# Attention and mixture of experts in one kernel: another order for the steps of each head pair

## The chip, the cores and the metric

One Trainium2 chip, one of its cores. The metric is the device time of one execution in microseconds (us), as the median of several runs. The kernel before takes 621.43 us (three runs, 620.74 to 623.72).

## What is computed

The reference, cut to what matters: an attention over 4 batches of 8 heads, 576 positions and 64 channels, with a position bias from a small network that is the same for all batches, and behind it a layer of 8 experts of which each token uses one.

```python
scores = scale * np.matmul(q, k.transpose(0, 1, 3, 2))     # q, k, v: (4, 8, 576, 64)
scores = scores + bias.transpose(2, 0, 1)[None, :, :, :]
attn = softmax(scores)
x = np.matmul(attn, v)  ->  (2304, 512)
e_idx = np.argmax(x @ w_gate, axis=1)
for e in range(8):
    mask = e_idx == e
    h = np.maximum(x[mask] @ w1[e], 0.0)                   # w1: (8, 512, 1024)
    out[mask] = gate_w[mask, None] * eom[mask, e, None] * (h @ w2[e])
```

## The kernel before, in words

The program has three stages, one behind the other: the position bias, the attention, and the experts. Each engine executes its instructions in the order in which the program emits them; nothing reorders them, and an instruction that waits holds up all that stand behind it on its engine.

**Attention.** The work goes by pairs of heads: 16 pairs, four to a batch. The code calls the index of the pair n (0 to 15, and 16 for what is left over). A pair is cut into small steps, and the order of the steps is written out by hand in four strings at the top of the file: ORDER (pairs 1 to 14), FIRST (pair 0), LAST (pair 15), END (what is left). A program loop walks through the string and emits one step per word. A minus behind a word means that the step belongs to the pair before, a plus to the next pair, two plus signs to the one after it. The words are:

- `s0` to `s4`: the score matmuls of one block of 128 queries (L833, into PSUM tiles `ps`, of which there are two; a block of two heads takes both, `s4` takes one). `m0` to `m4`: their softmax: VectorE adds the bias and finds the maximum (L845, into `e`), ScalarE takes the exponential (L850).
- `t00` to `t04`, `t10` to `t14`, `t20`, `t21`: TensorE turns pieces of `e` (L886, L898; into PSUM tiles `pt`, three of them), and the letter behind names the engine that copies the result to `et` (L890, L901): `a` is ScalarE, `d` is VectorE.
- `a0`, `a1`, `a2`: the products with the values (L918, one PSUM tile `pa`), with the copy to `xt` (L919) on the engine that the letter names.
- `k0` to `k2` and `h0` to `h2`: keys and queries of the next pair are turned (L810), copied in a high part (L813, ScalarE) and a low part (L815, VectorE, under `h`).
- `l`, `v`, `b`: loads of keys with queries (`nat`), values (`vt`) and the tail of the values (`vb`), issued on SyncE's queue. `z`, `c`, `g`: small copies on GpSimd: the queries of the last block into `q4` (L821), which `s4` reads, and pieces of values into `vz` (L803, L794), which `a0`, `a1`, `a2` read. The very first `t` step also emits the `c` of pair 0 (emit_t).
- `w` and `u`: one step of mixed-in work if there is any: the gate logits of a finished batch (emit_logits), the choice of its expert (emit_route), storing its rows of x (emit_x), and, for the first three batches, the sorting of the tokens by expert (route_group: L415 is its last matmul, L461 writes the indices `gidx`).

In pair 15 the experts begin to move in: `W` loads the first w1 (2 MB), `y` splits half a row block of it into a high part (ScalarE, L539) and a low part (GpSimd, L540), eight in all, `X` first emits what is left of route_group and then the three gathers of the first slot's 288 tokens (first_x, gather, L497: indirect DMAs of 96 rows of 2 KB on GpSimd's queue), and the fourth `y` emits the three gathers of the next slot. The first w2 (first_w2, another 2 MB, L483) is put at the head of the mixed-in work by `m3`. `x` turns a quarter of the gathered tokens (L515), which needs all three gathers.

**Experts.** Eight slots and more of 288 tokens each: matmuls with w1 (L1102) and w2 (L1123).

```python
for n in range(len(pairs) + 1):
    for op in orders.get(n, ORDER).split():
        name = op.rstrip("+-")
        m = n + op.count("+") - op.count("-")
```

Of the kernel before, what the change touches and what calls it, by code (L numbers as in the profile page):

```python
# [20 lines left out]
B, H, S, D = 4, 8, 576, 64  # L21
# [23 lines left out]


ORDER = (
    "l++ s0 b- c t10a- w t12a- m0 u t13d- k2+ s1 u t14a- m1 h2+ u t21d- a0d- w u w u w g- s2 z t20a- t01a t03a m2 u "
    "t02d u a2d- w s3 u k1+ k0+ t00a m3 u s4 w m4 u t04a h1+ h0+ u a1d- v+ t11d u "
)  # L50

FIRST = (
    "l++ s2 z m2 t01a t03a t02d s3 m3 t00a v+ s4 m4 t04a t11d"
)

LAST = (
    "b- B W s0 c t10a- u w t12a- m0 u t13d- u s1 t14a- m1 u t21d- a0d- w u s2 z t20a- g- m2 a1a- u t01a t03a w u y "
    "t02d u s3 y t00a m3 u X y t04d s4 y a2d- m4 w y t11d t13a y a0d u t14d t12a y y w t21d u t20d u "
)

END = (
    "t10a- x x a1d- x x a2d- "
)


BEGIN = {
    3: "k0", 4: "k1", 5: "k2 l", 13: "K0", 16: "K1", 17: "s00", 20: "K2",
    22: "s10 s01", 32: "s11", 35: "v",
}


ON_ACT = "210210000111121212102110310010201111"

# [1176 lines left out]
```

## Time and profile before

| what | value |
|---|---|
| median of three runs | 621.43 us |
| the profiled execution's own time | 626.37 us |
| its span, first to last instruction | 624.6 us |
| TensorE (PE) busy | 580.3 us, 93% |
| VectorE (DVE) busy | 410.8 us, 66% |
| ScalarE (ACT) busy | 362.0 us, 58% |
| GpSimd (POOL) busy | 105.6 us, 17% |
| the chain that ended last, share of TensorE | 79% |

The profile was taken in one execution, and times in it count from its first instruction. In that execution the bias lasts to about 82 us, the attention to about 381 us, the experts to the end. The clock of TensorE that a row gives as 1.00 is 2.4 GHz, as 0.50 it is 1.2 GHz.

### The profile page before, as it was taken

The page shows a single profiled execution, that of the slowest core. Times are in us where ns is not written, and L with a number is a line of the kernel's source. Part 1 is how long each engine was busy: PE and PEld are TensorE (multiplying, and loading weights), DVE is VectorE, ACT ScalarE, POOL GpSimd, SP SyncE. Part 2 cuts the span into 40 slices and gives each one's busy share as a digit, 9 for nine tenths or more (in the row PEclk, how much of TensorE's full clock was granted, in tenths as well). Part 3 has the DMA queues.
Part 4 walks back from the last instruction along what each step waited for, and adds up shares of the span by engine and source line. Part 5 has one row for each costly group of instructions (what it writes and reads, how often), then busy time and mean ns, then how long its engine had stood idle before and what let it go on. Part 6 is the DMA issues. An engine that isn't in the chain of part 4 may idle for free.

```text
span 624.6 us, 13990 instructions
## 1 busy us (share of the span) xinstructions
PE 580.3 (93%) x5294; PEld 472.9 (76%) x5294; DVE 410.8 (66%) x975; ACT 362.0 (58%) x773; POOL 105.6 (17%) x220
## 2 busy tenths in 40 slices
PE   5887899999999999999998979999999999999993
PEld 2333477767777667777676757999999999999993
DVE  6987567666876668766788644766778674655521
ACT  5796677666666676575657563544555455454510
POOL 1000011100011101011104272040404041331202
PEclk9997899999999999999999998999999999999998
DMA  6865653332133332233320565467566575747621
GB/s 144 217 175 143 171 112 68 67 69 57 36 111 76 67 69 58 81 73 67 69 79 28 173 209 171 147 204 240 159 217 199 169 205 174 227 145 236 181 76 44
DMA packets 94997, 81.40 MB, mean 130 GB/s; under 512 B 71319, under 2 KB 71575, under 8 KB 94920
## 3 DMA queue, kind: packets, MB, share of 16 engines
q1 hardware_dynamic: 88932, 66.05, 39.0%
q0 software_dynamic: 3232, 9.64, 4.8%
q10 hardware_dynamic: 2756, 4.72, 2.1%
q8 instruction: 43, 0.70, 0.5%
q14 instruction: 34, 0.28, 0.1%
HBM read 60.34 MB, written 9.50 MB: 112 GB/s over the span
## 4 chain that ended last, share of the span: by engine, by line
PE 79%; DVE 6%; DMA 4%; ACT 4%; issue 3%; POOL 2%; SPq 1%; POOLq 0%; DVEq 0%; ACTq 0%
PE p L1102 16%; PE p L1123 16%; PE pa L918 14%; PE ps L833 10%; PE pt L886 9%; PE pb L737 4%; PE pt L810 2%; DMA bias<-evl 2%; PE pt L515 1%; PE pt L1142 1%; PE pt L898 1%; PE pt L657 1%; DMA xg<-x_dram,gidx 1%; DVE hid L726 1%; DVE e L845 1%
## 5 line engine op out<-in xcount | busy, mean ns | idle before, releaser
L845 DVE CUSTOM_DVE_ANT_0 e<-ps,bias 128x576 f32<-128x576 f32 x144 | 103.9, 754 | 40.1 <-PE ps L833 34.6
L850 ACT ACTIVATE e<-e,nm 128x576 f32<-128x576 f32 x144 | 111.1, 780 | 10.0 <-DVE nm L845 10.0
L1102 PE MATMUL p<-x,w 128*128 128x288 f32 x768 | 105.8, 297 | 0.0
L1102 PEld LDWEIGHTS p<-x,w 128*128 128x128 f32 x768 | 102.8, 188 | 0.5 <-issue 0.4
L886 PE MATMUL pt<-kept,e 128*128 128x128 f32 x576 | 84.1, 280 | 3.6 <-DVE x L666 2.5
L890 ACT COPY et<-pt 128x512 f32<-128x512 f32 (+1 forms) x117 | 59.8, 534 | 42.4 <-PE pt L886 41.0
L886 PEld LDWEIGHTS pt<-kept,e 128*128 128x128 f32 x576 | 62.6, 141 | 20.0 <-issue 9.9
L1123 PE MATMUL p<-hh,w2h 128*128 128x288 f32 x256 | 77.3, 302 | 0.0
L1123 PE MATMUL p<-hl,w2h 128*128 128x288 f32 x256 | 75.6, 295 | 0.1
L1123 PE MATMUL p<-hh,w2l 128*128 128x288 f32 x256 | 75.3, 294 | 0.0
L918 PE MATMUL pa<-et,vt 128*64 128x256 f32 (+1 forms) x640 | 74.9, 360 | 0.0
L737 PE MATMUL pb<-hid,w2blk 128*32 128x288 f32 x576 | 47.9, 459 | 16.7 <-DVE hid L726 7.5
L918 PEld LDWEIGHTS pa<-et,vt 128*64 128x64 f32 x640 | 43.3, 139 | 22.7 <-issue 9.0
L1067 POOL DMA_INDIRECT out_dram<-y,sidx x22 | 26.4, 1198 | 180.5 <-DVE y L1145 154.2
L1104 ACT ACTIVATE hh<-p 128x288 fp32r<-128x288 f32 x64 | 26.3, 411 | 46.3 <-PE p L1102 30.8
L726 DVE TENSOR_SCALAR hid<-e,early 128x576 f32<-128x576 f32 x110 | 48.4, 514 | 7.1 <-PE pb L737 3.5
L737 PEld LDWEIGHTS pb<-hid,w2blk 128*32 128x32 f32 x576 | 19.4, 120 | 41.5 <-DVE hid L726 9.7
L833 PE MATMUL ps<-qt 64*128 64x288 f32 x256 | 47.8, 344 | 2.9 <-DVE nm L845 2.0
L1123 PEld LDWEIGHTS p<-hh,w2h 128*128 128x128 f32 x256 | 48.0, 188 | 0.6 <-issue 0.6
L487 DVE TENSOR_TENSOR w2l<-w2r,w2h 128x1024 fp32r<-128x1024 f32 x32 | 39.2, 1225 | 14.0 <-ACT w2h L486 12.5
L1123 PEld LDWEIGHTS p<-hl,w2h 128*128 128x128 f32 x256 | 48.1, 188 | 0.3 <-DVE hl L1105 0.3
L1123 PEld LDWEIGHTS p<-hh,w2l 128*128 128x128 f32 x256 | 48.2, 188 | 0.0
(222 smaller groups left out, 968.8 us busy)
## 6 DMA issues: line engine op xcount, KB each, us to landing
w1r<-in_moe_w_dram SPq DMA_DIRECT2D x36, 512.0 KB, 5.1
w2r<-in_moe_w_dram SPq DMA_DIRECT2D x36, 512.0 KB, 5.0
bias<-evh SPq DMA_DIRECT2D x16, 288.0 KB, 4.4
bias<-evl SPq DMA_DIRECT2D x16, 288.0 KB
vt<-in_v_dram SPq DMA_DIRECT2D x16, 288.0 KB, 3.4
nat<-in_k_dram SPq DMA_DIRECT2D x32, 128.0 KB, 3.6
nat<-in_q_dram SPq DMA_DIRECT2D x32, 128.0 KB, 2.6
x_dram<-x ACTq DMA_DIRECT2D x12, 256.0 KB, 2.0
```

The costliest lines, as they stand in the source:

```text
L487: V.tensor_tensor(out=lo, in0=src, in1=hi.bitcast(F32), op=ALU.subtract)
L726: V.tensor_scalar(out=to, in0=src, scalar1=bc[:, r:r + 1], scalar2=0.0, op0=ALU.add, op1=ALU.max,)
L737: nc.tensor.matmul(pb[32 * t:32 * t + 32, c, 0:288], lhsT=w2f, rhs=hids[t][:, c * 288:c * 288 + 288], start=True, stop=True,)
L833: nc.tensor.matmul(outs[hl][:, c, 0:288], lhsT=qs[p, S + 64 + qb * 128:S + 192 + qb * 128] if qb < 4 else q4[:, t, :], rhs=keys[p, c * 288 ...
L845: V.tensor_tensor_reduce(out=e.rearrange("p (a j) -> p a j", a=2), in0=ps[:, :, 0:n], in1=bias_ap.rearrange("p (a j) -> p a j", a=2), scal ...
L850: nc.scalar.activation(out=e, in_=e, func=ACTF.Exp, scale=-1.0, bias=nm, accum_out=sum_ap)
L886: nc.tensor.transpose(pt[:, n * 256 + j * 128:n * 256 + j * 128 + 128], es[j][:, (n0 + n) * 128:(n0 + n) * 128 + 128], ident,)
L890: copy(out=et[:, n0:n0 + nn, :].rearrange("p n s -> p (n s)"), in_=pt[:, 0:nn * 256])
L918: nc.tensor.matmul(pa[p:p + 64, 0:n], lhsT=values, rhs=weights, start=i == 0, stop=i == 4)
L1067: p = nc.gpsimd.indirect_dma_start(out=out, out_offset=bass.IndirectOffsetOnAxis(ap=idx, axis=0), in_=y[0:n], in_offset=None, bounds_check ...
L1102: nc.tensor.matmul(p1[:, 0:CH], lhsT=w[:, fs], rhs=x[:, c, :], start=n == 0, stop=n == 11)
L1123: nc.tensor.matmul(p2[:, 0:CH], lhsT=w[f // 2][:, f % 2, ds], rhs=x[f], start=n == 0, stop=n == 23)
```

## The change

The four strings are written anew; no step is added or dropped, and each step does what it did. The line numbers of the rest of the file fall by one. Shortened:

```diff
 ORDER = (
-    "l++ s0 b- c t10a- w t12a- m0 u t13d- k2+ s1 u t14a- m1 h2+ u t21d- a0d- w u w u w g- s2 z t20a- t01a t03a m2 u "
+    "b- w s0 u g- w k1+ k2+ m0 z h2+ a0a- h1+ t21d- u c t20a- u t13a- w t14a- s1 t11a- t10a- m1 w t12d- u "
+    "u l++ k0+ s2 m2 w h0+ w u a1a- s3 t00a m3 t04d u t02a s4 t03a m4 t01d a2a- v+ u "
...
 FIRST = (
-    "l++ s2 z m2 t01a t03a t02d s3 m3 t00a v+ s4 m4 t04a t11d"
+    "l++ t04d s2 t03a m2 t02d z t00a s3 m3 v+ s4 t01a m4 "
...
 LAST = (
+    "a1a- s3 m3 y t00a w t04d t02d s4 t10a t01d t03a y u m4 a2d- X u y y y a0d y t21d u t14a t13a y u u "
...
 END = (
-    "t10a- x x a1d- x x a2d- "
+    "x a1a- x x x a2a- "
```

What moves, in words. In pairs 1 to 14 all copies of `a0`, `a1`, `a2` go from VectorE to ScalarE. The keys of the next pair are turned right behind `s0` and in front of `s2`, no longer beside `s3`; `a0` comes in front of `s1`, and `a1` between `s2` and `s3`. All five `t1` steps of a pair are now emitted in the pair behind it. In pair 0 a `t` step comes first and the `q4` copies (`z`) behind it. In pair 15 `X` stands behind `s4`, `m4` and `a2`, where it stood ahead of `s4`, and the sorting of tokens has four steps left when `X` is reached, where it had none.

GpSimd at the start of the attention, before (`vz` and `et` are cleared, `q` is `q4`, of pair 0; then the values of pairs 0 and 1):

```order
L977 MEMSET vz_897 128x64
L821 CAST q_122<-qt_118 64x64 x2
L821 CAST q_122<-qs_120 64x64 x2
L803 COPY vz_895<-vt 64x64 x2
L803 COPY vz_896<-vt 64x64 x2
```

and now:

```order
L976 MEMSET vz_897 128x64
L802 COPY vz_895<-vt 64x64 x2
L820 CAST q_122<-qt_118 64x64 x2
L820 CAST q_122<-qs_120 64x64 x2
L793 COPY vz_897<-vb 64x64
```

The copies of values of pair 0 stand ahead of the `q4` copies of pair 0, which stood ahead of them.

ScalarE in pairs 2 and 3, from the last exponentials of a pair into the next, before (`e_139` is `m3`, `e_893` is `m4`, `e_136` is `m0`):

```order
L850 ACTIVATE e_139,sums<-e_139,nm 128x576 x2
L850 ACTIVATE e_893,sums_535<-e_893,nm 128x576
L890 COPY et<-pt 128x256
L890 COPY et<-pt 128x512 x2
L850 ACTIVATE e_136,sums<-e_136,nm 128x576 x2
```

and now:

```order
L849 ACTIVATE e_139,sums<-e_139,nm 128x576 x2
L889 COPY et<-pt 128x512 x2
L849 ACTIVATE e_893,sums_535<-e_893,nm 128x576
L918 COPY xt_1225<-pa 128x64
L812 CAST qt_119<-pt 128x384 x2
L849 ACTIVATE e_136,sums<-e_136,nm 128x576 x2
L918 COPY xt_1046<-pa 128x256
```

The copies of `a2` and `a0` (`xt`) and two castings of keys have come into this stretch.

GpSimd in pair 15, before (`w_1` is the low part of w1, written by a `y`; the first two DMA rows are the gathers of the first slot, the third those of the next):

```order
L540 TENSOR_TENSOR w_1_4856<-w1r_4679,w_0_4855 128x512
L540 TENSOR_TENSOR w_1_4856<-w1r_4680,w_0_4855 128x512
L497 DMA xg_4908<-x_dram,gidx_102 96x512 x2
L497 DMA xg_4909<-x_dram,gidx_102 96x512
L540 TENSOR_TENSOR w_1_4856<-w1r_4681,w_0_4855 128x512
L540 TENSOR_TENSOR w_1_4856<-w1r_4682,w_0_4855 128x512
L497 DMA xg_4909<-x_dram,gidx_102 96x512 x3
```

and now:

```order
L539 TENSOR_TENSOR w_1_4765<-w1r_4622,w_0_4764 128x512
L399 TENSOR_TENSOR ge<-ge 128x5x39
L401 TENSOR_TENSOR a_4808<-ge,kept 128x5x39 x2
L539 TENSOR_TENSOR w_1_4765<-w1r_4623,w_0_4764 128x512
L539 TENSOR_TENSOR w_1_4765<-w1r_4624,w_0_4764 128x512
L465 COPY ids_p<-ids_a 96x21
L496 DMA xg_4944<-x_dram,gidx_102 96x512 x2
L496 DMA xg_4945<-x_dram,gidx_102 96x512
L539 TENSOR_TENSOR w_1_4765<-w1r_4625,w_0_4764 128x512
L496 DMA xg_4945<-x_dram,gidx_102 96x512 x3
```

Three `y` steps and the last of the sorting stand ahead of the first gathers, where two `y` steps stood.

## Rows read from the trace of the kernel before

**Rows 1.** Windows: stretch and length, busy PE, PEld, DVE, ACT, POOL, PEclk, DMA, GB/s.

```profile
136.15:211.10 74.95, 73.02 (x712) 54.70 (x713) 52.98 (x139) 48.60 (x123) 7.69 (x35) 1.00 0.31 73
211.10:286.05 74.95, 73.01 (x712) 54.69 (x713) 52.98 (x139) 48.60 (x123) 7.63 (x35) 1.00 0.30 72
286.05:346.70 60.65, 55.14 (x529) 40.43 (x529) 45.38 (x142) 36.92 (x92) 10.77 (x36) 1.00 0.18 48
...
364.55:381.40 16.85, 13.31 (x99) 8.07 (x98) 5.90 (x15) 6.84 (x16) 12.02 (x11) 0.80 0.88 296
```

**Rows 2.** Chain of waits: start, length, what; the products a1 of two pairs.

```profile
119.54 2.31 PE pa L918 x20
...
136.15 2.31 PE pa L918 x20
```

**Rows 3.** Timeline of TensorE in one pair: start, length, tile, shape, count.

```profile
131.18 0.66 PE L886 MATMUL pt<-kept,e 128*128 128x128 f32 x4
131.77 0.40 PE L833 MATMUL ps<-qt 64*128 64x288 f32 x2
...
132.76 1.53 PE L886 MATMUL pt<-kept,e 128*128 128x128 f32 x12
134.14 0.55 PE L810 MATMUL pt<-kept,nat 128*128 128x128 f32 x3
134.62 0.40 PE L833 MATMUL ps<-qt 64*128 64x288 f32 x2
```

**Rows 4.** Groups by form: count, busy us, mean ns, idle before; copies of ScalarE.

```profile
L890 ACT COPY et<-pt 128x512 f32<-128x512 f32 x87 | 48.7, 591 | 41.7 <-PE pt L886 40.4 <-PE pa L918 0.8
L813 ACT CAST qt<-pt 128x384 fp32r<-128x384 f32 x48 | 21.5, 479 | 10.6 <-PE pt L810 10.6
L919 ACT COPY xt<-pa 128x256 f32<-128x256 f32 x1 | 0.4, 372 | 0.2 <-PE pa L918 0.2
```

**Rows 5.** Timeline at the start of the attention, in brackets the wait and its releaser.

```profile
75.25 0.52 POOL L821 CAST q<-qt 64x64 fp32r<-64x64 f32 x2
...
79.25 0.52 POOL L803 COPY vz<-vt 64x64 f32<-64x64 f32 x2 [2.89 <-DMA vt<-in_v_dram]
...
82.19 0.61 SPq L769 DMA_DIRECT2D nat<-in_q_dram  x1
...
84.36 0.52 PE L810 MATMUL pt<-kept,nat 128*128 128x128 f32 x3 [0.86 <-DMA nat<-in_q_dram]
```

**Rows 6.** Two windows of 2 us at the end of the bias, columns as before.

```profile
68.00:70.00 2.00, 1.16 (x20) 0.71 (x24) 0.78 (x3) 0.87 (x2) 0.00 (x0) 0.95 0.79 195
70.00:72.00 2.00, 2.00 (x24) 0.92 (x20) 0.00 (x0) 0.74 (x1) 0.00 (x0) 0.50 0.03 8
```

**Rows 7.** Timeline at the end of the attention, pair 15.

```profile
361.61 0.75 DVE L845 CUSTOM_DVE_ANT_0 e<-ps,bias 128x576 f32<-128x576 f32 x1
...
362.40 2.12 SPq L483 DMA_DIRECT2D w2r<-in_moe_w_dram  x4
...
364.93 0.78 ACT L850 ACTIVATE e<-e,nm 128x576 f32<-128x576 f32 x1 [0.24 <-DVE nm L845]
...
366.00 0.91 POOL L497 DMA_INDIRECT xg<-x_dram,gidx  x1 [0.30 <-issue]
...
368.36 0.62 PE L588 MATMUL pt<-xt,wgb 128*32 128x256 f32 x2 [0.87 <-DVE xt L919]
...
374.38 0.90 PE L515 MATMUL pt<-kept,xg 96*128 96x96 f32 x4 [1.95 <-DMA xg<-x_dram,gidx]
...
375.21 3.68 PE L918 MATMUL pa<-et,vt 128*64 128x256 f32 x16
...
379.68 1.06 PE L515 MATMUL pt<-kept,xg 96*128 96x96 f32 x6
...
380.67 0.27 PE L918 MATMUL pa<-et,vt 128*64 128x64 f32 x1
...
381.40 0.40 PE L1102 MATMUL p<-x,w 128*128 128x288 f32 x1
```

More of the change, by code (lines that the diff above doesn't have):

```diff
@@ L47 @@
 ORDER = (
-    "l++ s0 b- c t10a- w t12a- m0 u t13d- k2+ s1 u t14a- m1 h2+ u t21d- a0d- w u w u w g- s2 z t20a- t01a t03a m2 u "
-    "t02d u a2d- w s3 u k1+ k0+ t00a m3 u s4 w m4 u t04a h1+ h0+ u a1d- v+ t11d u "
+    "b- w s0 u g- w k1+ k2+ m0 z h2+ a0a- h1+ t21d- u c t20a- u t13a- w t14a- s1 t11a- t10a- m1 w t12d- u "
+    "u l++ k0+ s2 m2 w h0+ w u a1a- s3 t00a m3 t04d u t02a s4 t03a m4 t01d a2a- v+ u "
 )
 FIRST = (
-    "l++ s2 z m2 t01a t03a t02d s3 m3 t00a v+ s4 m4 t04a t11d"
+    "l++ t04d s2 t03a m2 t02d z t00a s3 m3 v+ s4 t01a m4 "
 )
 LAST = (
-    "b- B W s0 c t10a- u w t12a- m0 u t13d- u s1 t14a- m1 u t21d- a0d- w u s2 z t20a- g- m2 a1a- u t01a t03a w u y "
-    "t02d u s3 y t00a m3 u X y t04d s4 y a2d- m4 w y t11d t13a y a0d u t14d t12a y y w t21d u t20d u "
+    "B b- W c z s0 w w m0 a0a- g- u t21d- u t11a- t20a- t14a- s1 t10a- u t13a- u u m1 t12d- y w w s2 m2 w "
+    "a1a- s3 m3 y t00a w t04d t02d s4 t10a t01d t03a y u m4 a2d- X u y y y a0d y t21d u t14a t13a y u u "
+    "t20d t11d t12a "
 )
 END = (
-    "t10a- x x a1d- x x a2d- "
+    "x a1a- x x x a2a- "
 )
```

## The prediction

> **What bounds the kernel now.** I read the windows of the attention first, by stages. In each of the two middle batches TensorE is busy for 73.0 of 74.95 us at full clock, while VectorE has 53 and ScalarE 49 [rows 1]. TensorE is the bound there, and an order of steps can win only what TensorE stands idle: 1.93 us in each batch. In 286 to 347 us, where the sorting of tokens is mixed in, it stands idle for 60.65 − 55.14 = 5.51. At the end of the attention, 364.55 to 381.40, it stands idle for 16.85 − 13.31 = 3.54, and its mean clock is 0.80. Next I read the chain of waits. Two `a1` groups of neighbouring pairs without mixed-in work lie 136.15 − 119.54 = 16.61 us apart [rows 2], and in that stretch the timeline of TensorE has only short gaps. Last I read the timelines of both ends of the attention, where the change moves POOL's and SP's work. The experts keep their order. I count nothing for them.
>
> The sum is made against the profiled execution (own time 626.37, span 624.6). The median is 621.43, 4.94 lower. I take the difference from the sum off the median.
>
> **Pairs 1 to 14: −1.8 us.** No matmul is added or dropped. What changes is how often TensorE goes from turning `e` to other work. Four turnings took 131.77 − 131.18 = 0.59 us, and twelve with three of the keys behind them took 134.62 − 132.76 = 1.86 [rows 3]. So one costs (1.86 − 0.59) / 11 = 0.115, and a run of them costs 0.59 − 4 × 0.115 = 0.13 besides. The new order has five runs in a pair where there were six: 14 × 0.13 = 1.8. The bounds are 0 (the 0.13 may belong to the score matmuls behind it) and −1.8. I take −1.8 as the row gives it.
>
> The three copies of `a0`, `a1`, `a2` cost ScalarE 0.37 each [rows 4], 1.1 more per pair, and it has room: 48.6 of 74.95 in a batch. Whether each copy comes in time is a question of order. The tile `pa` exists once, so `a0` of a pair waits for the copy of `a2` of the pair before. From the last score matmul of `s4`, TensorE still has `t03` and `t01` (0.59 each), `a2` (381.40 − 380.67 = 0.73 [rows 7]), `s0` (132.76 − 131.77 = 0.99 [rows 3]) and six turnings of keys (6 × 0.115 + 0.13 = 0.82) ahead of `a0`, together 3.7. On the other side stand VectorE's pass (0.75) and ScalarE's exponential (0.78) [rows 7], the copy of `t03` (0.59) and the copy of `a2` (0.37) [rows 4]: 2.5, and 3.0 with an estimate of 0.5 for the hand-overs between engines, for which the row of the exponential shows 0.24 once. The slack is 0.7 us, so I cost this at nothing. If ScalarE comes later than that, TensorE waits in every pair (below). The other copies have slacks of 0.4 and more in the same reckoning.
>
> **Mixed-in work: −4.2 us.** The idle time of rows 1 that belongs to it is 1.93 × 2 + 5.51 = 9.4. It is mostly of the kind seen in pair 15: the logits' matmul stood for 0.87 us because VectorE's copy of `xt` was not there [rows 7]. In the new order `a0` and the `u` behind it are parted by turnings of keys or `e`, so some of these waits fall under other work. Others stay, since `w` still follows `a2` closely, and the sorting is a chain of small steps on four engines that no order shortens. Bounds: −9.4 and 0. I take something less than half, −4.2, because no row shows one of these steps in its new place.
>
> **Start: +3.0 us.** Now POOL copies the values of pair 0 first and waits there for their load until 79.25; the `q4` copies, which were through at 75.25 + 2 × 0.52, stand behind it [rows 5]. They end near 79.25 + 3 × 0.52 = 80.8. `s4` of pair 0 needs them, and the timeline has it at 79.0. TensorE has little else to do from about 78.0 and stands until 80.8. It can't make up for this by pushing on, since the keys of pair 2 (`k1`, `k2`) now stand right behind `s0` of pair 1. Their load is issued at 82.19, and TensorE got it at 84.36 after 0.86 us of waiting [rows 5]. By then four runs of turnings, 1.97 us, have been done before and won't have been now. So they come late by 2.0. If the idle time lowers the clock, more is lost: TensorE was busy for 1.16 of 2 us at 68 to 70, and the next window was granted 0.50, which is 1.2 GHz [rows 6]. Four to six us at half speed would cost another 2 to 3. Bounds +1.2 (the four runs fit elsewhere in part) and +5; I take +3.0, one us for a chance of the clock.
>
> The Trainium skill, page "TensorE: Matmul & The Clock Gate", section on the HAM clock gate, says that the throttled state is the default and that activity releases it; rows 6 agree in that 0.50 follows a half idle stretch, and by this rule the start would come out at +5 and the total at −5.9.
>
> **End: −4.9 us.** Before, the third gather was issued at 366.00, and TensorE stood for its tokens until 374.38, 1.95 us in the last wait alone. From there to 381.40 it ran at 1.2 GHz: `a1` took 379.68 − 375.21 = 4.47 [rows 7] where it takes 2.31 at full clock [rows 2], a loss of 2.16, and the ten turnings of tokens around it took (375.21 − 374.38) + (380.67 − 379.68) = 1.82, by half too long: 3.0 in all. Now `X` stands behind `s4` and `a2`, but `a0`, most of the last turnings and one more pair of steps fill TensorE until the first `x`. I count from the start of `a0` of pair 15. TensorE then has `a0` (2.31), five to six runs of turnings of up to 0.59 (3.2) and a step of logits (two of 0.62): the first `x` stands near 7.0. The sorting's last matmul is just ahead of `a0`, and the indices come a few small VectorE operations later, at 1.1 by estimate. Each issue takes POOL 0.91 [rows 7] and a pause of 0.3, so the third gather goes out at about 3.7. The load of w2 (2 MB) is issued some 5 us ahead of the first gather, where it was issued 1 us ahead. Before, it and the gathers landed together 374.38 − 362.40 = 12.0 us behind its issue. I take the gathers to land at 6 to 7, the load being drained by then. The 3.54 of idle time and the 3.0 of clock go. In their place come four short waits for copies (ends of sorting, `xt`, `t20`, and the single `pa`), each of the size of a copy of 0.37 to 0.59 [rows 4], 1.6 in all: −3.54 − 3.0 + 1.6 = −4.9. Bounds −6.5 and +1.6 (the gathers late, next part). On POOL three `y` and the sorting's last steps now stand ahead of the gathers; the splits of w1 behind them are needed only in the middle of the first slot, so their delay costs nothing.
>
> **Sum.** +3.0 − 1.8 − 4.2 − 4.9 = −7.9: a span of 616.7, and 621.43 − 7.9 = **613.5 us**.
>
> **The rivals.** *The gathers take as long as before.* The third took 374.38 − 366.00 = 8.4 us from issue to use [rows 7]. Issued at 3.7, it would be there at 12.1, five us behind the need, and TensorE would stand and lose its clock again for 3: the end becomes −6.5 + 1.6 + 5 + 3 = +3.1 and the total 0: 621.5 us. For it: the queues are loaded at a share of 0.88 there, 296 GB/s [rows 1]. Against it: the load of w2, which made them slow, now starts 4 us sooner in relation to them.
>
> The Trainium skill ("DMA: Bandwidth & Descriptors", "Queues, rings and completion order") says that a transfer's semaphore write lands only after every earlier write of the same DMA engine, across its queues. It fits the 8.4 us: the gathers then can't report before the 2 MB ahead of them. By the same rule an earlier load sets them free earlier, and what decides is when w2 is through. Another section of that page gives 2.0 us plus bytes over 436 GB/s for one transfer, an estimate of 2.5 us for a gather alone; by this no wait would be left.
>
> *The idle time only moves.* Mixed-in waits stay at 9.4 in other places, and the clock falls at the start (+5): 5 − 1.8 + 0 − 4.9 = −1.7, 619.7 us. For it: the sorting is a chain. Against it: the waits named in the trace are for copies.
>
> *ScalarE becomes late: slower.* If the exponential of `m4` and the castings of keys (two of 0.48 [rows 4], now ahead of `m0`) hold up the copy of `a2` or `a0` by more than the 0.7 us of slack, `a0` waits in each pair. For twice the distance from the slack, an overrun of 1.7 us, TensorE stands 1.0 us per pair: +14, 621.43 − 7.9 + 14 = 627.5 us. It decides from 0.7 us upward; at 1.3 the gain is gone. For it: three more copies on an engine whose exponentials come in bunches. Against it: ScalarE would be busy for 48.6 / 74.95 + 1.1 / 16.6 = 71% of its time.
>
> **How the numbers follow.** I give the forecast 0.50, the late gathers 0.15, the moved idle time 0.17, the late ScalarE 0.13, and 0.05 to what I don't see. The forecast's own range is 606.5 (start +1.2 and nearly all mixed-in idle time gone) to 619.5 (start +5, end −3). With the two middle rivals the range runs to 623.0; left out are the late ScalarE and a part of the rest. About 0.5%, 3.1 us, is what a measurement of this kernel can tell from no change. Faster by more (under 618.3): the forecast but for its upper edge and a third of the moved idle time, with some of the rest, 0.57. Within it: the late gathers and most of the moved idle time, 0.27. Slower: the late ScalarE and some of the rest, 0.16.
>
> **What would show it.** In the profile of the changed kernel: idle time of TensorE for POOL's `q` near 79 to 81 us and a wait of `k1` for `nat` behind it; two `a1` of neighbouring pairs 16.5 us apart; a batch of 73.5 to 74.5 us; no wait of L515 for `xg`, and clock 1.00 to the first expert matmul. The forecast is wrong if L918 waits for ScalarE's `xt` in each pair, if `xg` is waited for, or if the windows with sorting have their 5.5 us of idle time still.

## The result, and the profile after

The changed kernel takes 602.98 us (median of four runs, 601.00 to 604.23), the one before 622.4 us beside it: a ratio of 0.969, 95% interval 0.965 to 0.973. The forecast was 613.5 with a range of 606.5 to 623: the direction was right, the gain of 19.4 us is two and a half times the 7.9 that I had summed, and the time lies below the range.

The profiled execution of the changed kernel took 601.0 us (span 599.2), that of the kernel before 626.37: 25.4 apart, 6 more than the medians, so terms read from the two traces come out some 6 us too large in all. Of these 6, 2.7 lie in the bias stage, whose last matmul ended at 73.64 us before and at 70.97 after with the same instructions, and some 3 in the clock at the end of the attention (below). Busy times of the page, after:

```profile
PE 565.7 (94%) x5294; PEld 471.1 (79%) x5294; DVE 395.6 (66%) x936; ACT 374.6 (63%) x812; POOL 106.2 (18%) x220
```

TensorE has the same 5294 matmuls, and is *busy* for 14.6 us less (580.3 before). Some of this is the clock, but much of the gain can't have been in any idle time that the profile showed. To see where, I cut both attentions at the first score matmul of `s4` of each pair. The windows of the kernel before, columns as in [rows 1]: pair 1, pair 3, pairs 4 to 7 (a batch with mixed-in work), pairs 12 to 14 (with sorting), pair 15 with the stretch to the first expert matmul.

```profile
79.00:94.33 15.33, 14.47 (x144) 11.63 (x145) 9.83 (x26) 11.62 (x29) 2.03 (x9) 1.00 0.50 108
110.96:127.59 16.63, 16.63 (x167) 12.77 (x165) 11.29 (x29) 11.72 (x30) 1.57 (x7) 1.00 0.30 64
127.59:202.52 74.93, 73.00 (x711) 54.71 (x710) 52.97 (x139) 48.59 (x123) 7.69 (x35) 1.00 0.31 72
277.48:340.84 63.36, 59.07 (x563) 43.50 (x562) 47.35 (x145) 40.06 (x100) 11.01 (x38) 1.00 0.24 60
340.84:381.40 40.56, 35.09 (x309) 24.48 (x309) 21.06 (x59) 22.65 (x53) 19.51 (x26) 0.92 0.59 193
```

The same five of the changed kernel:

```profile
78.25:95.16 16.91, 16.86 (x141) 13.05 (x141) 8.53 (x22) 10.61 (x26) 2.04 (x9) 0.90 0.44 97
111.33:127.50 16.17, 16.17 (x168) 12.81 (x166) 9.95 (x26) 12.87 (x33) 1.57 (x7) 1.00 0.30 66
127.50:197.96 70.46, 70.31 (x713) 54.58 (x711) 47.50 (x127) 52.84 (x135) 7.63 (x35) 1.00 0.32 77
268.40:323.70 55.30, 55.28 (x555) 42.61 (x553) 42.67 (x128) 40.32 (x103) 7.67 (x31) 1.00 0.27 68
323.70:355.90 32.20, 30.91 (x328) 23.12 (x326) 24.27 (x68) 23.45 (x57) 19.95 (x30) 1.00 0.60 187
```

Five readings. Pair 1 is longer by 1.6 us. A pair without mixed-in work falls from 16.63 to 16.17, though TensorE counts as busy for all of it in both. A batch falls by 4.5 us (of which 4 × 0.46 = 1.8 are the pairs), pairs 12 to 14 by 8.1, and their idle time, 1.93 and 4.29, is gone. The end falls by 8.4, at a clock of 1.00 where it was 0.92. The experts take 243.2 and 243.3 us.

A useful figure for what follows is the *price of a batch's mixed-in work*: the batch less four plain pairs. Before it is 74.93 − 4 × 16.63 = 8.4 us, after 70.46 − 4 × 16.17 = 5.8, for the same matmuls. And here is why the idle column didn't show it: the logits of `a0`, in the timeline of TensorE before,

```profile
137.86 0.60 PE L918 MATMUL pa<-et,vz 128*64 128x256 f32 x4
138.39 1.22 PE L588 MATMUL pt<-xt,wgb 128*32 128x256 f32 x8
140.07 0.44 PE L618 MATMUL pt<-kept,ls 128*128 128x128 f32 x2 [0.46 <-ACT ls L611]
```

and after, where nine turnings of `e` stand between `a0` and them:

```profile
133.65 0.60 PE L917 MATMUL pa<-et,vz 128*64 128x256 f32 x4
134.19 0.74 PE L897 MATMUL pt<-kept,e 128*64 128x128 f32 x5
...
135.29 0.64 PE L587 MATMUL pt<-xt,wgb 128*32 128x256 f32 x8
135.86 0.44 PE L885 MATMUL pt<-kept,e 128*128 128x128 f32 x2
```

From the first of the eight matmuls to the next work 1.68 us pass, from 138.39 to 140.07, where 0.57 are enough unhindered (135.29 to 135.86). Of the 1.11 us between, 0.46 show as idle time; that is the next step's wait for ScalarE's copy of the logits, `ls`. The rest is the logits' own wait for `xt`. It counts as busy, since a group that waits in its middle is drawn out: 1.22 us where it takes 0.64.

### The profile page after: what moved, and what is told of

Same layout as the page of the kernel before. It is cut to its first block, busy times and chain, and to the rows that moved or that the text cites. A ratio compares the mean times of both kernels' runs of the same rounds, so it can differ in the third digit from the quotient of the medians.

```text
span 599.2 us, 13978 instructions
## 1 busy us (share of the span) xinstructions
PE 565.7 (94%) x5294; PEld 471.1 (79%) x5294; DVE 395.6 (66%) x936; ACT 374.6 (63%) x812; POOL 106.2 (18%) x220
## 4 chain that ended last, share of the span: by engine, by line
PE 81%; issue 2%; DVE 1%; DMA 1%; POOL 1%; ACT 1%; SPq 1%; POOLq 0%
PE p L1101 16%; PE p L1122 16%; PE pa L917 14%; PE ps L832 12%; PE pt L885 11%; PE pt L809 3%; PE pt L897 2%; PE pt L656 2%; PE pt L1141 1%; PE pt L514 1%; PE pt L587 1%; SPq L749 1%; DMA vt<-in_v_dram 1%; DMA xg<-x_dram,gidx 1%; POOL out_dram L1066 0%
## 5 line engine op out<-in xcount | busy, mean ns | idle before, releaser
L889 ACT COPY et<-pt 128x512 f32<-128x512 f32 (+1 forms) x111 | 57.9, 557 | 36.2 <-PE pt L885 36.0
L885 PE MATMUL pt<-kept,e 128*128 128x128 f32 x576 | 79.6, 279 | 0.7 <-ACT et L889 0.4
L917 PE MATMUL pa<-et,vt 128*64 128x256 f32 (+1 forms) x640 | 73.2, 354 | 0.2 <-DVE xt L918 0.2
L736 PE MATMUL pb<-hid,w2blk 128*32 128x288 f32 x576 | 45.8, 437 | 16.7 <-DVE hid L725 7.6
L1066 POOL DMA_INDIRECT out_dram<-y,sidx x22 | 26.3, 1198 | 173.5 <-DVE y L1144 147.2
L1103 ACT ACTIVATE hh<-p 128x288 fp32r<-128x288 f32 x64 | 26.3, 411 | 45.7 <-PE p L1101 39.7
```

Source lines behind the costliest of these rows:

```text
L736: nc.tensor.matmul(pb[32 * t:32 * t + 32, c, 0:288], lhsT=w2f, rhs=hids[t][:, c * 288:c * 288 + 288], start=True, stop=True,)
L885: nc.tensor.transpose(pt[:, n * 256 + j * 128:n * 256 + j * 128 + 128], es[j][:, (n0 + n) * 128:(n0 + n) * 128 + 128], ident,)
L889: copy(out=et[:, n0:n0 + nn, :].rearrange("p n s -> p (n s)"), in_=pt[:, 0:nn * 256])
L917: nc.tensor.matmul(pa[p:p + 64, 0:n], lhsT=values, rhs=weights, start=i == 0, stop=i == 4)
L1066: p = nc.gpsimd.indirect_dma_start(out=out, out_offset=bass.IndirectOffsetOnAxis(ap=idx, axis=0), in_=y[0:n], in_offset=None, bounds_check ...
```

## Experiments

Times are medians; what they are held against is 602.98 for the changed kernel and 622 to 623 for the one before. Single executions of one kernel spread by 3 us and more (19 of the kernel before: 620.0 to 627.6), so I give windows of the traces where they say more: between pairs 2 and 14 two executions of the same instructions agree to a few hundredths of a microsecond.

**Copies on VectorE again.**

```diff
-a0a- ... a1a- ... a2a-
+a0d- ... a1d- ... a2d-
```

> The changed kernel, with the copies of a0, a1, a2 in pairs 1 to 14 on VectorE again, every step in the new order. Theory 1 (the gain comes from the order of the steps on TensorE, and the engine of the copies is of no weight): within 2 us of the changed kernel, a pair without mixed-in work 16.2 to 16.4 us. Theory 2 (ScalarE's earlier copies carry the gain): a0 and the logits wait for VectorE, a batch goes back from 70.4 towards 75 us, and the kernel loses 6 us or more.

611.17 us, ratio to the kernel before 0.982 (0.977 to 0.987). A plain pair and a batch:

```profile
115.00:131.73 16.73, 16.38 (x167) 12.79 (x166) 10.93 (x29) 12.24 (x30) 1.57 (x7) 1.00 0.29 64
131.73:204.35 72.62, 71.12 (x712) 54.48 (x711) 51.36 (x139) 50.38 (x123) 7.62 (x35) 1.00 0.31 75
```

The first line is a plain pair, the second pairs 4 to 7. That is 0.56 more per pair, 14 × 0.56 = 7.8 of the 8.2 us. The amount is theory 2's, the path is not: the logits cost no more than before. Where it sits, in TensorE's timeline and in VectorE's:

```profile
122.76 0.88 PE L885 MATMUL pt<-kept,e 128*128 128x128 f32 x6 [0.35 <-DVE qs L814]
```

```profile
120.14 0.55 DVE L814 TENSOR_TENSOR qs<-pt,qt 128x384 fp32r<-128x384 f32 x1
121.82 0.42 DVE L918 COPY xt<-pa 128x256 f32<-128x256 f32 x1 [1.13 <-PE pa L917]
122.16 0.55 DVE L814 TENSOR_TENSOR qs<-pt,qt 128x384 fp32r<-128x384 f32 x1
```

Nobody waits for the copy. VectorE stands idle in front of it for 1.13 us until its product is done, and behind it stands the low part of the keys. That could have started at 120.69, when the one before it ended; it starts at 122.16, and must be taken before a `pt` tile is free for the turnings. The price of mixed-in work, from this trace's batch of 72.62 us, is 72.62 − 4 × 16.73 = 5.7, unchanged.

**The same, with the low part of the keys ahead of the copy.**

```diff
-h2+ a0a- h1+ ... a1a- ... a2a-
+h2+ h1+ a0d- ... a1d- ... a2d-
```

> The changed kernel with the copies of a0, a1, a2 on VectorE, as in the run that cost 8 us, but with h1 (the low part of the keys that k1 has turned) ahead of the copy of a0 instead of behind it. Theory 1 (on VectorE the copy of a0 waits 2.3 us for its product, the low part of the keys waits behind it, and the turnings behind a0 have no free tile): the 0.56 us per pair go again, a pair takes 16.1 to 16.3 us, the kernel 601 to 605. Theory 2 (VectorE is late by its sum of work): a pair stays at 16.6 to 16.8 us and the kernel at 609 to 612.

605.41 us, ratio 0.972 (0.968 to 0.975), and the pair is as short as with ScalarE:

```profile
116.58:132.74 16.16, 16.16 (x167) 12.80 (x166) 10.92 (x29) 12.15 (x30) 1.58 (x7) 1.00 0.30 66
```

So the second theory falls: VectorE was not late by its amount of work. What counts is which instruction waits in front of which. (The median is 2.4 us above the changed kernel's and just above theory 1's 605; the intervals overlap. The profile of this kernel reached `s4` of pair 0 at 82.31 us, that of the changed kernel at 78.25; the bias, by the same instructions, had ended 4.3 us later. From there on they keep step but for pair 1.)

**The kernel before with its copies on ScalarE.**

```diff
-a0d- ... a2d- ... a1d-
+a0a- ... a2a- ... a1a-
```

> The kernel before, with the copies of a0, a1, a2 in pairs 1 to 14 on ScalarE, nothing else. The same step backwards in the changed kernel cost 8 us and 0.56 us per pair. Theory 1 (the relief of VectorE is the gain, whatever the order): a pair without mixed-in work falls from 16.62 to 16.0 to 16.3 us, the kernel gains 5 to 10 us. Theory 2 (the relief and the order need each other: in the old order nothing on TensorE stands behind those copies on VectorE): a pair stays within 0.2 us of 16.62 and the kernel within 3 us.

625.76 us, ratio 1.004 (1.002 to 1.007). The plain pair, and pairs 4 to 7:

```profile
108.46:125.08 16.62, 16.62 (x166) 12.78 (x165) 10.20 (x26) 12.55 (x33) 1.57 (x7) 1.00 0.31 64
125.08:200.82 75.74, 72.95 (x712) 54.69 (x710) 48.93 (x127) 52.00 (x135) 7.69 (x35) 1.00 0.30 72
```

Theory 2: nothing is won. The batch is even 0.8 us longer, and the median 3.1 above the kernel before beside it. By the old strings the keys' low part did not stand behind those copies. The engine of the copies is no gain of its own; in the new order it keeps the order from costing 0.56.

**One stretch of turnings more.**

```diff
-l++ k0+ s2 m2
+l++ s2 k0+ m2
```

> The changed kernel, with the turning of one piece of keys (k0) moved from behind the twelve turnings of e to behind s2, so that it stands alone between score matmuls and values: one more stretch of full-size matmuls per pair, every instruction as before. Theory 1 (TensorE loses about 0.15 us each time it goes from small-tile work, scores or values, into full-size turnings and out again, and much of the 0.45 us per pair is one such stretch less): a pair goes from 16.17 to 16.3 to 16.4 us, the kernel loses 1.5 to 3.5 us. Theory 2 (the 0.45 us are waits for copies alone): 16.15 to 16.2 us per pair.

607.78 us, ratio 0.975 (0.971 to 0.978).

```profile
116.58:133.01 16.43, 16.43 (x168) 12.95 (x166) 9.95 (x26) 12.91 (x33) 1.59 (x7) 1.00 0.29 65
```

Three turnings moved, nothing added, no idle time, and 0.26 us more in a plain pair, as theory 1 had it. Single starts in the traces say what the 0.26 is made of: inside a stretch one turning starts 0.109 us behind the other; the first takes 0.165, and from the last to the next score or value 0.203 go by (the four of [rows 3] make 0.165 + 2 × 0.109 + 0.203 = 0.59). That is 0.15 for a stretch between scores and values. Next to `s4`, which uses all 128 rows as the turnings do, the new order shows no such loss: the ten turnings ahead of it take 1.07 us, and of the eight behind it only the last, ahead of values, pays. The other 0.11 is in the scores and turnings around it (`s2` 1.13 where it had 0.99 to 1.00 us), a wait below what the view shows. In pairs 4 to 7 the move cost 0.35 us in all (70.81 against 70.46), not four times 0.26, and in pairs 2 to 14 together 1.9. The median lost 4.8, more than theory 1's 1.5 to 3.5; in its profile pair 1 took 19.19 us at a mean clock of 0.82, and what the rest is made of was not followed up.

**Mixed-in work right behind the products.**

```diff
-a0a- h1+ ... t13a- w t14a- ... h0+ w u a1a- s3
+a0a- w h1+ ... t13a- t14a- ... h0+ u a1a- w s3
```

> The changed kernel, with one step of mixed-in work moved to stand right behind a0 and one right behind a1 (where they stood in the kernel before), as many steps as ever. Theory 1 (the waits left because other work now stands between a product and the logits that need its copy): at the ends of three batches the logits wait twice for xt, 0.6 to 1.1 us each, and the kernel loses 3 to 7 us; the idle time of a batch goes from 0.15 back to 1 us or more. Theory 2 (they left because ScalarE copies at once): no more than 1 us is lost.

618.89 us, ratio 0.993 (0.991 to 0.996): 16 us lost, over twice as much as theory 1 had. The plain pair is untouched, the batch is not:

```profile
115.38:131.54 16.16, 16.16 (x167) 12.80 (x165) 9.94 (x26) 12.88 (x33) 1.58 (x7) 1.00 0.30 66
131.54:207.79 76.25, 73.40 (x712) 55.98 (x711) 47.78 (x127) 53.23 (x135) 7.69 (x35) 0.98 0.29 71
```

The price of mixed-in work is 76.25 − 4 × 16.16 = 11.6 against 5.8. The logits wait again: 138.23 to 139.35, 1.12 us where 0.57 are enough. The larger part I had not foreseen: in pair 6 the storing of x comes sooner after the choice of experts, on which it depends, and TensorE stands behind it,

```profile
178.52 0.66 PE L897 MATMUL pt<-kept,e 128*128 128x128 f32 x4 [2.13 <-DVE x L665]
```

while VectorE waits for POOL:

```profile
177.77 0.69 DVE L665 TENSOR_TENSOR x<-pt,rec 128x512 f32<-128x512 f32 x1 [3.17 <-POOL rec L644]
```

Pair 6 takes 22.1 us instead of 17.7; behind the wait the granted clock is at 1.2 GHz for a part of it (0.50 from 180 to 182 us), which makes the 0.98 of the batch. So theory 1, with a second path that it did not have: a step of mixed-in work needs distance from the copy that it reads and from the step before it.

**Moving mixed-in work in the kernel before.** Two tries. First, out of the place behind `a0` and `a2` into the next steps:

```diff
-a0d- w u w u w g- s2 z t20a- t01a t03a m2 u t02d u a2d- w s3 u
+a0d- u u g- s2 z t20a- w t01a w t03a m2 w u t02d u a2d- s3 u w
```

> The kernel before, with the three steps of mixed-in work behind a0 and the one behind a2 moved some steps on, nothing else. Theory 1 (waits of logits and sorting behind the copies are a part of their own, some 8 us of idle time in pairs 4 to 14): a batch falls from 74.95 to 73 to 74 us, and the kernel gains 3 to 6 us on the one before. Theory 2 (the gain of the change is in the order of scores, turnings and values): no change beyond 1 us.

624.24 us, ratio 1.003 (1.000 to 1.006). Second, spread out:

```diff
-k2+ s1 u t14a- ... a0d- w u w u w g- s2 z t20a- t01a t03a m2 u ... a2d- w s3 u k1+ k0+
+k2+ s1 u w t14a- ... a0d- u u g- s2 z t20a- w t01a t03a m2 w u ... a2d- s3 u k1+ k0+ w
```

> The kernel before, its six steps of mixed-in work per pair spread so that none stands right behind a0, a1 or a2 and no two stand side by side; nothing else. In the run with three of them in one stretch, the wait of the logits was gone, but the scores of block 3 waited 0.7 us for VectorE instead. Theory 1 (the places of mixed-in work are a gain of their own in either order): a batch falls from 74.95 to 72 to 74 us, the kernel gains 3 to 6 us. Theory 2 (in the old order every place delays a softmax or a copy that TensorE needs soon, and the gain needs the new order's slack on VectorE): within 2 us of the kernel before.

626.44 us, ratio 1.005 (1.002 to 1.008). Pairs 4 to 7 of the two:

```profile
127.52:203.44 75.92, 73.40 (x711) 54.79 (x710) 52.45 (x139) 49.49 (x123) 7.74 (x35) 1.00 0.30 71
```

```profile
127.39:203.75 76.36, 72.81 (x712) 54.48 (x710) 52.29 (x139) 49.27 (x123) 7.74 (x35) 1.00 0.30 71
```

Prices of 9.4 and 9.8 us against 8.4. The logits' wait did go (0.57 us for the eight in both), but other work came late instead: in the first, the scores of block 3 took 1.66 us where they need 0.99. So theory 1 falls for these two placements; both kernels are, if anything, slower (1.6 and 3.3 us in the medians). Whether some other placement would do in the old order was not tried.

**The old end.**

```diff
-"B b- W c z s0 ... s4 t10a t01d t03a y u m4 a2d- X u ..."
+"b- B W s0 t11d- c t10a- ... u X y t04d s4 y a2d- m4 ..."
```

> The changed kernel, with the order of the kernel before in pair 15 and behind it (X and the gathers ahead of s4, with no step of the sorting left over but those that X finds), and one t1 step of pair 14 put at its head, since pairs 1 to 14 now leave it over. Theory 1 (the place of the gathers and of the sorting is a gain of its own): pair 15 and the stretch to the first expert matmul take 38 to 40 us against 32.2, and the kernel loses 5 to 8 us. Theory 2 (most of that gain was the clock that fell in one profile of the kernel before): 36 to 37 us, the kernel loses 3 to 5 us. If the place is of no weight: under 1 us.

607.08 us, ratio 0.973 (0.969 to 0.978): 4.1 us lost in the medians, 7.8 in the trace. The medians give theory 2's amount; the trace gives theory 1's, but the clock fell in it (0.91), as in the profile of the kernel before:

```profile
323.68:363.70 40.02, 35.05 (x327) 24.88 (x326) 24.98 (x71) 23.45 (x55) 23.14 (x32) 0.91 0.59 191
```

Its gathers, and TensorE's wait for them:

```profile
344.13 2.12 SPq L481 DMA_DIRECT2D w2r<-in_moe_w_dram  x4
...
348.72 0.92 POOL L495 DMA_INDIRECT xg<-x_dram,gidx  x1 [0.30 <-issue]
...
356.05 1.46 PE L513 MATMUL pt<-kept,xg 96*128 96x96 f32 x5 [1.60 <-DMA xg<-x_dram,gidx]
```

and the changed kernel's own:

```profile
340.41 2.13 SPq L482 DMA_DIRECT2D w2r<-in_moe_w_dram  x4
...
344.60 1.95 PE L917 MATMUL pa<-et,vt 128*64 128x256 f32 x16 [0.19 <-DVE xt L918]
...
346.09 1.03 POOL L496 DMA_INDIRECT xg<-x_dram,gidx  x1 [0.39 <-DVE fi L461]
...
348.65 0.91 POOL L496 DMA_INDIRECT xg<-x_dram,gidx  x1 [0.30 <-issue]
...
351.73 0.30 PE L514 MATMUL pt<-kept,xg 96*128 96x96 f32 x1 [0.39 <-DMA xg<-x_dram,gidx]
```

The third gather goes out at the same time in both, and its tokens are used 7.3 us later in the old end, 3.1 in the new. What differs ahead of it is the load of w2: 2.0 us before the first gather there (346.15), 5.7 here. The Trainium skill's rule ("DMA: Bandwidth & Descriptors", "Queues, rings and completion order"), that a semaphore write lands only after every earlier write of its DMA engine, across queues, agrees with both. The other four profiles with the old end fit too: there the load is issued 1.0 us ahead of the first gather, and the third gather's tokens are used 6.7 to 8.4 us after its issue. That the load's place alone makes the difference was not tried by itself.

**The start.** Four kernels, each the changed one with edits at its start. In it TensorE waits for POOL's `q4` copies:

```profile
78.25 0.40 PE L832 MATMUL ps<-qt,q 128*128 128x288 f32 x1 [2.85 <-POOL q L820]
```

The first puts `z` ahead of the first `t` step:

```diff
-l++ t04d s2 t03a m2 t02d z t00a
+l++ z t04d s2 t03a m2 t02d t00a
```

> The changed kernel, with the q4 copies of pair 0 put ahead of its first t step again (that is, ahead of the copies of values that wait for their load). Theory 1 (the start pays for POOL's wait, and for the clock that falls behind it): TensorE's 2.8 us of waiting for q at 78 to 81 us go, and the clock stays at 1.00 there; pair 1 falls from 16.9 us to 15.3 to 16.2, and the kernel gains 1 to 4 us on the changed one. Theory 2 (the keys of pair 2 set the start, since their load comes no sooner): TensorE waits for nat instead, and the time stays within 1 us.

605.07 us, ratio 0.973 (0.968 to 0.977): no gain. POOL is waited for no more, the keys of pair 2 are, as theory 2 had it:

```profile
82.01 0.30 PE L809 MATMUL pt<-kept,nat 128*128 128x128 f32 x1 [0.82 <-DMA nat<-in_k_dram]
84.22 1.30 PE L809 MATMUL pt<-kept,nat 128*128 128x128 f32 x5 [1.92 <-DMA nat<-in_q_dram]
```

and in this profile the granted clock fell to 1.2 GHz behind it (0.84 in the mean of pair 1), pair 1 taking 20.98 us. The second leaves `z` and issues the four small loads of gate weights later:

```diff
-for hl in range(2): for i, w in enumerate((wg, wog)): nc.sync.dma_start(out=wgb[...])
 for n in range(len(pairs) + 1):
+    if n == 2: the same four loads
```

> The changed kernel, with the four small loads of gate weights, which stand on SP's queue ahead of the keys of pair 2, issued at the start of pair 2 instead. They took 2.7 us of the queue. Theory 1 (the start waits for nat, and nat for the queue): the keys are there 2 to 3 us sooner, pair 1 takes 15.3 to 16.5 us without a lower clock behind it, and the kernel gains 1 to 4 us. Theory 2 (POOL's wait for the values sets the start): the values come sooner too, since their load stands ahead of the four; no change beyond 1 us.

603.67 us, ratio 0.968 (0.965 to 0.972): nothing, as POOL is still waited for (2.83 us). The third does both:

> As the run before this one, without the order of its own for pair 1: gate weights later and the q4 copies first. Theory 1 (the two waits are all that the start pays): a gain of 1 to 4 us on the changed kernel, about as much as with the order of its own. If the keys still come late, it gains less than 1 us, and TensorE waits for nat.

601.05 us, ratio 0.965 (0.961 to 0.968), 1.9 less than the changed kernel, and TensorE still waits 0.87 us for `nat` in its trace. The fourth turns `k1` and `k2` later in pair 1 besides:

```diff
+SECOND: m0 z a0a- t21d- ... l++ k0+ h0+ k1+ h1+ k2+ h2+ s2
-orders = {0: FIRST, ...}
+orders = {0: FIRST, 1: SECOND, ...}
```

> The changed kernel with three edits at its start: the gate weights loaded at pair 2, the q4 copies of pair 0 ahead of its first t step, and in pair 1 alone the keys k1 and k2 turned behind k0, ahead of s2. Theory 1 (the start of the changed kernel costs 3 to 4 us, in POOL's wait for values and in the keys' wait for their load, and each edit alone only passes the wait on to the other): no wait of TensorE over 1 us between 75 and 95 us, pair 1 at 15.2 to 16.0 us against 16.9 to 17.9, and the kernel gains 2 to 4 us on the changed one. Theory 2 (the start has its time from the clock, which falls there in any case): within 1 us.

599.94 us (599.61 to 601.56), ratio 0.963 (0.960 to 0.967), the fastest kernel of this study. Its pair 1:

```profile
77.82:94.04 16.22, 15.93 (x140) 12.06 (x141) 8.99 (x24) 12.06 (x30) 2.03 (x9) 1.00 0.45 99
```

Pair 1 is 0.2 us longer than theory 1 had, and no wait of TensorE there is over 0.93 us. So theory 1 in the main: taking one wait away alone won nothing, and both together are worth about 3 us. That is an estimate, since the interval of the ratio overlaps that of the changed kernel slightly (0.960 to 0.967 against 0.965 to 0.973).

## Why the forecast was too small

**Start, +3.0: about the right size, in part by another path.** The bias ends at other times in each execution, so I count from its last matmul to the end of pair 1. The last matmuls before, and after:

```profile
72.23 1.41 PE L737 MATMUL pb<-hid,w2blk 128*32 128x288 f32 x12
69.80 1.18 PE L736 MATMUL pb<-hid,w2blk 128*32 128x288 f32 x16
```

From their ends to 94.33 and 95.16 it is 20.7 and 24.2 us: 3.5 more, or 4.0 with the 0.46 that pair 1 wins like the others. The other three profiles with the old start have 20.6 to 21.1, five more with the new one 24.1 to 26.3, and the last two kernels of the experiment on the start 22.0 and 21.6. The wait for POOL's `q4` came (2.85 us). The late keys, 2.0 of my 3.0, did not come in the changed kernel. TensorE ran at 1.2 GHz for a while behind its wait for POOL, the chance for which I had added one us, and then turned the keys without a wait:

```profile
80.00:82.00 2.00, 2.00 (x14) 1.67 (x13) 0.66 (x2) 1.35 (x3) 0.00 (x0) 0.50 0.66 151
...
82.44 1.01 PE L809 MATMUL pt<-kept,nat 128*128 128x128 f32 x6
```

The wait for `nat` shows only where the one for `q` is taken away.

**Pairs, −1.8: mis-sized.** The step counted runs of turnings at 0.13 each and took everything else as unchanged. The measured term is 16.63 − 16.17 = 0.46 per pair, over 14 pairs 6.4 us. Single starts of matmuls tell where it sits. One stretch fewer between scores and values is 0.15 of it, close to the 0.13 that I had. Another 0.22 are three places inside stretches of the old order where a turning, or the first score behind one, starts 0.06 to 0.08 us late; the new order has one such place, of 0.02. The remaining 0.1 lies in and beside `s4` and behind `a0`. Such waits are below what the idle column shows. For two of the three the semaphores name what ended them, a copy of a `pt` tile on ScalarE. This one ends at 124.10, and the turning behind it starts at 124.16:

```profile
123.52 0.59 ACT L901 COPY et<-pt 128x512 f32<-128x512 f32 x1 [1.88 <-PE pt L898]
```

What stands behind the third stays open. So does one more change that I had not listed: four `t` steps of a pair copy on VectorE in either order, but `t13`, `t21`, `t02`, `t11` before and `t21`, `t12`, `t04`, `t01` after. What this is worth alone was not tried.

**Mixed-in work, −4.2 with bounds −9.4 and 0: the step that failed most.** Its lower bound rests on my sentence that an order of steps can win only what TensorE stands idle. That sentence is wrong. In pairs 4 to 14 the kernel won 340.84 − 127.59 − (323.70 − 127.50) = 17.1 us; less 11 × 0.46 for the pairs, 12.0 are left. The idle time there was 8.2 (1.93 in each of two batches and 4.29 in pairs 12 to 14) and is 0.3 now; the other 4 us were waits inside groups that count as busy, as the logits' rows above show. By single starts, the 2.6 us by which the price of a batch fell (8.4 to 5.8) are 1.5 in the logits' 24 matmuls, 1.0 in the 20 that store x, and 0.3 in those of `ls`, less 0.2 in turnings. The wait behind the storing in the kernel before was for VectorE:

```profile
186.81 0.44 PE L886 MATMUL pt<-kept,e 128*128 128x128 f32 x2 [0.83 <-DVE x L666]
```

I halved the idle time because no row showed a step in its new place; nearly all of it went. The run with two steps moved back shows that in the new order their place is what counts: it gave back all of this and more. In the old order two other places won nothing, so the gain belongs to the order and the places together. Where it is divided between pairs and mixed-in work is a convention, since 0.46 was measured in plain pairs only.

**End, −4.9: near, but by luck.** The whole of pair 15 and the end won 8.4 in the traces. Some 3 of that is the clock, which fell in the profile of the kernel before. My −4.9 had 3.0 of clock in it too, from that one execution, and I took it off a median; without it the forecast was −3.54 + 1.6 = −1.9. In the profiles of two kernels with the same end (the copies on ScalarE, the first of the moved mixed-in work) the clock did not fall there:

```profile
340.94:376.90 35.96, 32.24 (x309) 23.06 (x309) 20.28 (x58) 22.92 (x54) 18.42 (x26) 1.00 0.56 177
341.86:378.43 36.57, 32.25 (x309) 23.06 (x309) 20.72 (x59) 22.28 (x52) 19.04 (x26) 1.00 0.57 179
```

Against them the new end wins 3.8 and 4.4, twice my −1.9. The wait of 1.95 us for tokens is not in them either (0.31 and 0.29 at that place); their idle time of 3.7 and 4.3 us, 1.3 in the changed kernel, lies mostly in other waits. A third profile with that end, of the second try, took 41.2 us at a mean clock of 0.88. Counted from `a0`, the first gather went out at 1.5 (I had 1.1), the third at 4.05 (3.7; my own terms, 1.1 + 2 × 1.21, make 3.5), the first turning of tokens came at 6.4 (7.0), and the last wait for them was 0.39 us, where I had none.

With these sizes the sum is +4.0 − 6.4 − 12.0 − 4.1 = −18.5; the medians say −19.4. The terms come from single traces, and the start alone differs by 2 us between profiles, so an agreement within 1 us is partly luck. My range was too narrow on the fast side for the same reason as the sum: its edge of 606.5 let nearly all of the mixed-in idle time go, and nothing beyond it. (Its other edge is added up wrongly: with +5 at the start and −3 at the end the terms give 617.4, not 619.5.)

**The rivals.** The gathers did not take as long as before (3.1 us against 8.4 [rows 7]). The idle time did not merely move. ScalarE was not late: the copy of `a2` ends at 114.94 and the next `a0` starts at 115.70, a slack of 0.76 where I had 0.7. A danger of the new order that I did not have was on VectorE: there a copy of `a0` that waits for its product would have held up what stands behind it, at 0.56 us a pair.

## What to carry to other kernels

Idle time is no upper limit for what a better order can win: a group of matmuls that waits in its middle counts as busy, so compare the same group's length from start to next start where it waits and where it doesn't. On an engine that works in order, ask of each instruction that waits for a long product what ready work stands behind it and whose buffer that work frees; moving either one of the two was enough here. Mixed-in steps want distance both from the copy they read and from their own predecessor. A wait with two causes, as at this kernel's start, may show a gain only when both are taken away. And a loss that one execution shows, such as a fallen clock, may not be in the median that the sum is taken off.

## What the runs showed of the hardware

A stretch of full 128 × 128 matmuls between matmuls that use 64 rows or 64 columns cost 0.15 us besides its matmuls (0.165 for the first, 0.203 for the last, 0.109 each between). In the new order the side of a stretch that faces `s4`, which uses all rows, cost nothing; in the old order the first of two turnings behind `s4` took 0.165 all the same. I had counted a change of the kind of work. That the change of the shape is what counts fits the new order, but no run tried it alone.
